# Sliding-window attention: block-diagonal scores in the tile mode of the values, and both next to each other

## The chip, the cores and the metric

The kernel runs on one core of one Trainium2 chip. The metric is the device time of one execution, in microseconds (us); less is better. The granted TensorE clock is 1.00. Repeated executions of one kernel mostly agree within about 0.1%.

## The reference

Four blocks follow each other: attention, feed-forward over tokens, and both again. Only the attention matters here. It has 2048 positions, 32 heads of 32 elements, and every query sees eight keys: its own position and the seven at distance 2, 4, ... 14 before it.

```python
def _A_ref(x, wqkv, wo):
    H = 32; Dh = D // H
    W, dil = 8, 2
    q, k, v = ...                        # x @ wqkv, split into heads
    idx = pos[:, None] - (jnp.arange(W) * dil)[None, :]
    kg, vg = k[:, :, idx_c, :], v[:, :, idx_c, :]      # the 8 keys and values of each query
    logits = jnp.einsum("bhsd,bhswd->bhsw", q, kg) * Dh ** -0.5     # masked where idx < 0
    o = jnp.einsum("bhsw,bhswd->bhsd", _softmax(logits), vg)
    return o.reshape(B, S, D) @ wo

x = x + _A_ref(_layernorm(x), A_wqkv, A_wo)
x = x + _B_ref(_layernorm(x), ...)       # feed-forward; then both once more
```

## The kernel before

Positions are split into even and odd ones (`c`), so that the eight keys of a query are neighbours. Four heads (`g`) and one parity make a unit `u`, 16 units per layer; half a unit is a *visit*, 32 visits per layer, numbered 0 to 31. In each visit TensorE computes the scores of half a unit, the values (probabilities times v, and their row sums) of the half unit before it, and two of the four 512-column chunks of q or k of the next unit. In visits 30 and 31 there is no next unit, and two output projections each take the place of the chunks.

TensorE's order within a visit is fixed by the program:

```python
for vis in range(2 * NU):
    u, b = divmod(vis, 2)
    ...                                             # cut: weight loads
    in_order(scores, u, b)
    for n in range(2):
        if n and vis:
            in_order(values, *divmod(vis - 1, 2), v, oT)
        if u + 1 < NU:
            in_order(qk_chunk, u + 1, wts, *chunks[2 * b + n])
        else:
            in_order(out_proj, 0, 2 * b + n, oT, wo, res, xa[li], h2)
in_order(values, NU - 1, 1, v, oT)
for c, i in order[4:]:
    out_proj(c, i, oT, wo, res, xa[li], h2)
```

The scores use array tiles of 32 rows by 64 columns: 32 rows since a head has 32 elements, 64 keys, 72 queries. The values use tiles of 128 rows (keys) by 32 columns (elements of a head). The chunks and projections use the whole array.

```python
def scores(u, b):
    ...
    for i in range(HB):
        for r in range(2):
            for h in range(HG):                     # one head per row tile
                mm = nc.tensor.matmul(ss[h // 2][r * HK:(r + 1) * HK, h % 2, i * HW:(i + 1) * HW],
                                      lhsT=k[hp, lo:lo + HK], rhs=q[hp, lo:lo + HW], start=True, stop=True)
    for n in range(2):
        nc.scalar.activation(out=pc[...], in_=ss[n][:, :, 0:HB * HW], func=ACT.Exp, scale=scale, bias=shift[:])
    for r in range(2):                              # keep the band, write it into Pm
        nc.vector.tensor_tensor(out=pm[rp, :, ...], in0=pc[rp], in1=mk, op=ALU.mult)

def values(u, b, v, oT):
    acc = a_tile()                                  # one buffer of two PSUM banks
    ...                                             # cut: matmuls of v and of ones with Pm, into acc
    nc.scalar.activation(out=rd[:], in_=acc[:, 1, :], func=ACT.Ln)
    nc.scalar.activation(out=rd[:], in_=rd[:], func=ACT.Exp, scale=-1.0)
    nc.vector.tensor_tensor(out=oT[g][...], in0=acc[:, 0, :], in1=rd[:], op=ALU.mult)   # frees acc

def qk_chunk(u, wts, part, n):
    ...                                             # cut: eight matmuls of 128x512 into ps
    if n == 0: nc.scalar.copy(out=dst[:, lo:lo + 512], in_=ps[:])
    else:      nc.vector.tensor_copy(out=dst[:, lo:lo + 512], in_=ps[:])

def out_proj(c, i, oT, wo, res, dst, h2):
    xr = x2("xr")
    nc.sync.dma_start(out=xr[:], in_=res(c, i))     # the residual
    xn = x2("xn")
    for n in range(NDC):
        ...                                         # cut: eight matmuls of 128x512 into ps (two buffers in all)
        nc.vector.tensor_tensor(out=xn[:, xs_], in0=ps[:], in1=xr[:, xs_], op=ALU.add)   # frees ps
    nc.sync.dma_start(out=rows(dst, c, i), in_=xn[:])
    ...                                             # cut: statistics (VectorE), normalisation (ScalarE)
```

PSUM has `m` tiles (two buffers of one bank, for chunks and projections), `s` tiles (two of two banks, scores) and `acc` (one of two banks, values).

The softmax here doesn't subtract the row's maximum and nothing guards it: scores larger than these inputs give would overflow.

Of the kernel before, what the change touches and what calls it, by code (L numbers as in the profile page):

```python
# [14 lines left out]
P = 128  # L15
H = 32
DH = 32
# [8 lines left out]
def kernel(  # L26
# [31 lines left out]
    NW2 = 4  # L58
    HF = FT // NW2
    KW = P + W  # L60
    HK = P // 2
    HW = HK + W
    PAD = W
    SHIFT = 14.0
    assert D == H * DH and NT == 16 and NI == 8 and NG == 8 and HG == 4
    scale = float(DH) ** -0.5
# [20 lines left out]
    def s_tile():  # L87
        return pss.tile([P, 2, 512], FP32, name="s", tag="s")
# [13 lines left out]
    def x2(name, shape=None, dt=BF16):  # L102
        return x2p.tile(shape or [P, D], dt, name=name, tag="x2")
# [18 lines left out]
    nc.vector.memset(shift[:], -SHIFT)  # L122
    ones = const.tile([P, DH], BF16, name="ones")
    nc.vector.memset(ones[:], 1.0)
    band = const.tile([P, HW], BF16, name="band")
    nc.gpsimd.memset(band[:], 1.0)
    for r in range(2):
        hb_ = band[r * HK:(r + 1) * HK]
        nc.gpsimd.affine_select(out=hb_, in_=hb_, compare_op=ALU.is_ge, fill=0.0, base=0,
                                pattern=[[1, HW]], channel_multiplier=-1)  # L130
        nc.gpsimd.affine_select(out=hb_, in_=hb_, compare_op=ALU.is_ge, fill=0.0, base=W - 1,
                                pattern=[[-1, HW]], channel_multiplier=1)
    b1_bf = const.tile([P, FT], BF16, name="b1_bf")
    b2_bf = const.tile([P, NI, DIL], BF16, name="b2_bf")
    b1_sb = const.tile([P, FT], FP32, name="b1_sb")
# [9 lines left out]
        return nc.vector.tensor_copy(out=b2_sb[:], in_=b2_bf[:])  # L145

    hT = pers.tile([P, KD, S], BF16, name="hT")
    qT = [pers.tile([P, S + PAD], BF16, name=f"qT{n}") for n in range(2)]
    kT = [pers.tile([P, S], BF16, name=f"kT{n}") for n in range(2)]
    Pm = [pers.tile([P, HG, NI, KW], BF16, name=f"Pm{n}") for n in range(2)]  # L150
    def zero_fill():
        for t in qT:
            nc.vector.memset(t[:, S:S + PAD], 0.0)
        for t in Pm:
            nc.vector.memset(t[0:HK, :, :, HW:KW], 0.0)
            r = nc.vector.memset(t[HK:P, :, :, 0:HK], 0.0)
        return r

    xa = [dram.tile([S, D], BF16, name=f"xa{li}") for li in range(2)]
# [187 lines left out]
    def qk_chunk(u, wts, part, n):  # L347
        g, c = divmod(u, DIL)
        ps = m_tile()
        lo = c * SC + n * 512  # L350
        for kt in range(KD):
            mm = nc.tensor.matmul(ps[:], lhsT=wts[part][:, kt, (g % 2) * P:(g % 2 + 1) * P], rhs=hT[:, kt, lo:lo + 512],  # L352
                                  start=(kt == 0), stop=(kt == KD - 1))
        dst = (qT, kT)[part][g % 2]
        if n == 0:
            nc.scalar.copy(out=dst[:, lo:lo + 512], in_=ps[:])
        else:
            nc.vector.tensor_copy(out=dst[:, lo:lo + 512], in_=ps[:])
        return mm

    last_pe = [None]
# [2 lines left out]
        with tc.issue_after(last_pe[0].ins) if last_pe[0] is not None else nullcontext():  # L364
            last_pe[0] = f(*args)

    HB = NI // 2

    def scores(u, b):
        g, c = divmod(u, DIL)  # L370
        q, k, pm = qT[g % 2], kT[g % 2], Pm[u % 2]
        ss = [s_tile() for _ in range(2)]
        for i in range(HB):
            for r in range(2):
                lo = c * SC + (b * HB + i) * P + r * HK
                for h in range(HG):
                    hp = slice(h * DH, (h + 1) * DH)
                    mm = nc.tensor.matmul(ss[h // 2][r * HK:(r + 1) * HK, h % 2, i * HW:(i + 1) * HW],  # L378
                                          lhsT=k[hp, lo:lo + HK], rhs=q[hp, lo:lo + HW], start=True, stop=True)
        pc = pcp.tile([P, HG, HB, HW], BF16, name="pc", tag="pc")  # L380
        for n in range(2):
            nc.scalar.activation(out=pc[:, 2 * n:2 * n + 2].rearrange("p h t k -> p h (t k)"), in_=ss[n][:, :, 0:HB * HW],  # L382
                                 func=ACT.Exp, scale=scale, bias=shift[:])
        for r in range(2):
            rp = slice(r * HK, (r + 1) * HK)
            mk = band[rp].unsqueeze(1).unsqueeze(1).to_broadcast([HK, HG, HB, HW])
            nc.vector.tensor_tensor(out=pm[rp, :, b * HB:(b + 1) * HB, r * HK:r * HK + HW], in0=pc[rp], in1=mk, op=ALU.mult)  # L387
        return mm

    def values(u, b, v, oT):  # L390
        g, c = divmod(u, DIL)
        pm = Pm[u % 2]
        acc = a_tile()
        hb = NI // 2
        t0 = b * hb
        for i in range(-1 if b else 0, hb):
            t = t0 + i
            for h in range(HG):
                hp = slice(h * DH, (h + 1) * DH)
                lhs = v[c][t][:, g * P + h * DH:g * P + (h + 1) * DH]  # L400
                if i < 0:
                    nc.tensor.matmul(acc[hp, 0, 0:W], lhsT=lhs, rhs=pm[:, h, t, P:KW], start=True, stop=False,
                                     skip_group_check=True)
                else:
                    w = KW if i < hb - 1 else P
                    nc.tensor.matmul(acc[hp, 0, i * P:i * P + w], lhsT=lhs, rhs=pm[:, h, t, 0:w],  # L406
                                     start=(t == 0), stop=(i == hb - 1), skip_group_check=True)
        for h in range(HG):
            hp = slice(h * DH, (h + 1) * DH)
            nc.tensor.matmul(acc[hp, 1, :].rearrange("p (t q) -> p t q", q=P), lhsT=ones[:], rhs=pm[:, h, t0:t0 + hb, 0:P],  # L410
                             start=True, stop=False, skip_group_check=True)
        s0 = t0 - 1 if b else 0
        ns = t0 + hb - 1 - s0
        o0 = (s0 + 1 - t0) * P
        for h in range(HG):
            hp = slice(h * DH, (h + 1) * DH)
            dst = acc[hp, 1, :].rearrange("p (t q) -> p t q", q=P)[:, o0 // P:o0 // P + ns, 0:W]
            mm = nc.tensor.matmul(dst, lhsT=ones[:], rhs=pm[:, h, s0:s0 + ns, P:KW], start=False, stop=True,
                                  skip_group_check=True)
        rd = x2("rd", [P, 512], FP32)  # L420
        nc.scalar.activation(out=rd[:], in_=acc[:, 1, :], func=ACT.Ln)
        nc.scalar.activation(out=rd[:], in_=rd[:], func=ACT.Exp, scale=-1.0)  # L422
        lo = c * SC + t0 * P
        nc.vector.tensor_tensor(out=oT[g][:, lo:lo + hb * P], in0=acc[:, 0, :], in1=rd[:], op=ALU.mult)  # L424
        return mm

    def load_wo():
# [99 lines left out]
    for li in range(2):  # L527
        first = li == 0
        v = [[None] * NI for _ in range(DIL)]
        for c, i in order:  # L530
            v[c][i] = vhp.tile([P, D], BF16, name="v", tag="vh")
        wv = load_wv()
        if first:
            start_up(v, wv)
            wts = [None, None]
            chain_("SP", load_qk, 0, wts)
            res = lambda c, i: xin_v[c, i]
        else:
            fill_wv(wv, 0)
            fill_wv(wv, 1)  # L540
            wts = [None, None]
            load_qk(0, wts)
            for i in range(NI):
                for c in range(DIL):
                    v_proj(v, c, i, wv, (0, 1))
            res = lambda c, i: rows(xb, c, i)
        oT = [gop.tile([P, S], BF16, name="oT", tag="go") for _ in range(NG)]
        h2 = [[None] * NI for _ in range(DIL)]
        chunks = [(0, 0), (0, 1), (1, 0), (1, 1)]
        last_pe[0] = None  # L550
        for part, n in chunks:
            in_order(qk_chunk, 0, wts, part, n)
        wo = None
        for vis in range(2 * NU):
            u, b = divmod(vis, 2)
            if b == 0 and u + 1 < NU and (u + 1) % (2 * DIL) == 0:
                wts = [None, None]
                load_qk((u + 1) // (2 * DIL), wts)
            if vis == 2 * NU - 6:
                wo = load_wo()  # L560
            in_order(scores, u, b)
            for n in range(2):
                if n and vis:
                    in_order(values, *divmod(vis - 1, 2), v, oT)
                if u + 1 < NU:
                    in_order(qk_chunk, u + 1, wts, *chunks[2 * b + n])
                else:
# [4 lines that stand above are left out]
        g = [None] * NFB  # L572
        for fb in range(NFB):
            gemm1(fb, h2, g)
        if first:
            ln_exp_table()
        for i in range(NI):
            w2t = load_w2(i)
            for c in range(DIL):
                gemm2(c, i, w2t, g, xa[li], rows(xb, c, i) if first else out_v[c, i], first)  # L580
# [30 lines left out]
```

## Time and profile before

Median 1300.6 us of three runs (1300.58 to 1300.79). From the page of the profile, busy time of each engine, and below it the chain of work that ended last. PE is TensorE, PEld its weight loads, DVE VectorE, ACT ScalarE, POOL GpSimd, and SPq the queue of SyncE; a number after x is a count.

```profile
PE 1279.1 (99%) x9240; PEld 582.0 (45%) x9398; DVE 392.9 (30%) x654; ACT 386.0 (30%) x628; POOL 1.7 (0%) x11
...
PE 96%; DVE 2%; issue 1%; ACT 0%; DMA 0%; SPq 0%; another core or an unknown queue 0%
```

TensorE is the limit everywhere. What can be gained in attention is not idle time, for there is hardly any in the records, but the time that TensorE spends between matmuls. To see it, read the starts in the timeline. This is one visit, TensorE alone; the columns are start (us), duration of the piece (us), engine, line, operation, output and inputs, and the number of instructions.

```profile
152.98 0.38 PE L352 MATMUL m<-hT,wqk 128*128 128x512 bf16 x1
153.29 0.34 PE L378 MATMUL s<-qT,kT 32*64 32x72 bf16 x32
153.78 1.67 PE L352 MATMUL m<-hT,wqk 128*128 128x512 bf16 x7 [0.16 <-issue]
155.39 0.19 PE L402 MATMUL acc<-Pm,v 128*32 128x8 bf16 x4
...
155.99 1.90 PE L352 MATMUL m<-hT,wqk 128*128 128x512 bf16 x8
157.82 0.34 PE L378 MATMUL s<-qT,kT 32*64 32x72 bf16 x32
```

L378 is the scores, L352 a chunk, L402 the first line of the values. From scores to scores this visit takes 4.53 us; the mean of visits 1 to 28 is 4.5216 us. (The first of the eight matmuls at 153.78 is one of the few records missing from the trace.) Matmuls of a chunk start 216 ns apart, but the scores start 0.31 us after the last matmul of the chunk before them (152.98 to 153.29), and so do the values: 93 ns are lost each time TensorE goes from the whole array into small tiles. Coming back costs a similar time: in the next visit, where that record is there, the last score matmul and the next chunk start 126 ns apart, though groups of eight scores follow each other every 33 ns, and the last ones start only 9 to 11 ns after the last matmul of the group before. The Trainium skill, "TensorEngine Tiling (Array Packing)", Tiling Modes, says that changing the tiling mode drains the array. A visit enters and leaves small tiles twice.

The groups of VectorE (DVE) and ScalarE (ACT) in the stage: after the shapes come the count, busy us, mean ns of one, and the idle time before them with its cause.

```profile
L387 DVE TENSOR_TENSOR Pm<-pc,band 64x1152 bf16<-64x1152 bf16 x128 | 96.2, 752 | 65.1 <-ACT pc L382 63.1
...
L424 DVE TENSOR_TENSOR oT<-acc,rd 128x512 bf16<-128x512 f32 x64 | 44.0, 687 | 39.7 <-ACT rd L422 39.7
...
L358 DVE CAST qT<-m 128x512 bf16<-128x512 f32 x32 | 21.8, 682 | 75.4 <-PE m L352 75.4
```

VectorE has two masks, one oT and one cast in a visit, about 2.9 of 4.52 us, and it waits for others: there is slack.

### The profile page before, as it was taken

The page shows a single profiled execution, that of the slowest core. Times are in us where ns is not written, and L with a number is a line of the kernel's source. Part 1 is how long each engine was busy: PE and PEld are TensorE (multiplying, and loading weights), DVE is VectorE, ACT ScalarE, POOL GpSimd, SP SyncE. Part 2 cuts the span into 40 slices and gives each one's busy share as a digit, 9 for nine tenths or more (in the row PEclk, how much of TensorE's full clock was granted, in tenths as well). Part 3 has the DMA queues.
Part 4 walks back from the last instruction along what each step waited for, and adds up shares of the span by engine and source line. Part 5 has one row for each costly group of instructions (what it writes and reads, how often), then busy time and mean ns, then how long its engine had stood idle before and what let it go on. Part 6 is the DMA issues. An engine that isn't in the chain of part 4 may idle for free.

```text
span 1298.5 us, 20885 instructions
## 1 busy us (share of the span) xinstructions
PE 1279.1 (99%) x9240; PEld 582.0 (45%) x9398; DVE 392.9 (30%) x654; ACT 386.0 (30%) x628; POOL 1.7 (0%) x11
## 2 busy tenths in 40 slices
PE   9999999999999999999999999999999999999998
PEld 4444444444444444444444444444444444444443
DVE  7346667820000022322300666688000000111111
ACT  5457666521111110000023677765211111000000
POOL 0000000000000000000000000000000000000000
PEclk9999999999999999999999999999999999999999
DMA  8620113443222235555432100044422222334320
GB/s 236 133 77 21 35 34 111 150 145 91 65 80 77 57 105 143 130 154 140 130 81 65 35 21 27 24 145 157 129 65 84 78 59 80 104 106 140 112 91 33
DMA packets 195818, 121.69 MB, mean 94 GB/s; under 512 B 37904, under 2 KB 177424, under 8 KB 195728
## 3 DMA queue, kind: packets, MB, share of 16 engines
q1 hardware_dynamic: 195728, 120.36, 32.7%
q8 instruction: 73, 1.20, 0.4%
q14 instruction: 17, 0.14, 0.0%
HBM read 96.48 MB, written 16.78 MB: 87 GB/s over the span
## 4 chain that ended last, share of the span: by engine, by line
PE 96%; DVE 2%; issue 1%; ACT 0%; DMA 0%; SPq 0%; another core or an unknown queue 0%
PE m L352 17%; PE s L515 15%; PE s L472 15%; PE acc L472 7%; PE m L472 7%; PE m L515 7%; PE acc L515 7%; PE m L445 7%; PE m L337 4%; PE m L255 4%; PE acc L406 1%; PE s L378 1%; PE acc L410 1%; DVE xn L447 1%; DVE bn L180 0%
## 5 line engine op out<-in xcount | busy, mean ns | idle before, releaser
L472 PEld LDWEIGHTS <-w 128*128 128x128 bf16 x1792 | 175.4, 98 | 211.4
L515 PEld LDWEIGHTS <-w 128*128 128x128 bf16 x1792 | 175.3, 98 | 211.4
L352 PE MATMUL m<-hT,wqk 128*128 128x512 bf16 x963 | 231.0, 380 | 7.9 <-issue 7.0
L472 PE MATMUL s<-h,w 128*128 128x512 bf16 x878 | 201.3, 379 | 0.8
L515 PE MATMUL s<-g,w 128*128 128x512 bf16 x884 | 199.3, 379 | 0.7
L518 DVE SCALAR_TENSOR_TENSOR xo<-s,b_sb,xs 128x512 bf16<-128x512 f32 x32 | 24.0, 751 | 540.7 <-PE s L515 529.1
L352 PEld LDWEIGHTS <-wqk 128*128 128x128 bf16 x1024 | 90.5, 98 | 108.7 <-issue 12.9
L387 DVE TENSOR_TENSOR Pm<-pc,band 64x1152 bf16<-64x1152 bf16 x128 | 96.2, 752 | 65.1 <-ACT pc L382 63.1
L445 PE MATMUL m<-wo,oT 128*128 128x512 bf16 x498 | 111.5, 379 | 0.9
L382 ACT ACTIVATE pc<-s,shift 128x576 bf16<-128x576 f32 x128 | 87.8, 737 | 59.9 <-PE s L378 59.9
L472 PE MATMUL acc<-h,w 128*128 128x512 bf16 x440 | 103.1, 379 | 0.5
L515 PE MATMUL acc<-g,w 128*128 128x512 bf16 x436 | 99.6, 379 | 0.5
L472 PE MATMUL m<-h,w 128*128 128x512 bf16 x438 | 98.5, 379 | 0.5
L515 PE MATMUL m<-g,w 128*128 128x512 bf16 x436 | 98.3, 379 | 0.6
L174 ACT ACTIVATE ln<-mv,eps 128x1 f32<-128x1 f32 x64 | 18.9, 295 | 227.5 <-DVE mv L182 222.2
L479 ACT ACTIVATE g<-s,b_sb 128x1024 bf16<-128x1024 f32 x28 | 31.2, 1114 | 166.9 <-PE s L472 155.2
L445 PEld LDWEIGHTS <-oT 128*128 128x128 bf16 x512 | 49.4, 98 | 59.7 <-issue 1.3
L255 PE MATMUL m<-wv,hT 128*128 128x512 bf16 x250 | 55.6, 379 | 1.0 <-ACT hT L249 0.7
L424 DVE TENSOR_TENSOR oT<-acc,rd 128x512 bf16<-128x512 f32 x64 | 44.0, 687 | 39.7 <-ACT rd L422 39.7
L337 PE MATMUL m<-wv,hT 128*128 128x512 bf16 x251 | 55.2, 379 | 0.3
L447 DVE TENSOR_TENSOR xn<-m,xr 128x512 bf16<-128x512 f32 x64 | 44.0, 688 | 8.0 <-PE m L445 6.5
L180 DVE BATCH_NORM_STATS2 bn<-xn 128x6 f32<-128x512 bf16 x64 | 44.4, 693 | 1.4
(59 smaller groups left out, 604.9 us busy)
## 6 DMA issues: line engine op xcount, KB each, us to landing
w<-in_B_w_dram SPq DMA_DIRECT2D x56, 512.0 KB, 3.8
w<-in_B_w_dram SPq DMA_DIRECT2D x64, 448.0 KB, 4.7
wqk<-in_A_wqkv_dram SPq DMA_DIRECT2D x16, 512.0 KB, 5.9
xa<-xn SPq DMA_DIRECT2D x32, 256.0 KB, 2.0
xs<-xa SPq DMA_DIRECT2D x32, 256.0 KB, 3.2
wv<-in_A_wqkv_dram SPq DMA_DIRECT2D x8, 512.0 KB, 5.6
wo<-in_A_wo_dram SPq DMA_DIRECT2D x8, 512.0 KB, 4.9
xr<-in_A_x_dram SPq DMA_DIRECT2D x16, 256.0 KB, 2.9
```

Of the source, the lines that this page charges most:

```text
L180: nc.vector.bn_stats(out=s[:, cc, :], in_=x[:, cc * 512:(cc + 1) * 512])
L255: r = nc.tensor.matmul(pss_[k, n][:], lhsT=hT[:, kt, cols(*order[k])], rhs=wv[n][kt // 4][:, kt % 4, :], start=(kt == 0), stop=(kt == KD - 1))
L337: nc.tensor.matmul(ps[:], lhsT=hT[:, kt, cols(c, i)], rhs=wv[n][kt // 4][:, kt % 4, :], start=(kt == 0), stop=(kt == KD - 1))
L352: mm = nc.tensor.matmul(ps[:], lhsT=wts[part][:, kt, (g % 2) * P:(g % 2 + 1) * P], rhs=hT[:, kt, lo:lo + 512], start=(kt == 0), stop=(kt = ...
L382: nc.scalar.activation(out=pc[:, 2 * n:2 * n + 2].rearrange("p h t k -> p h (t k)"), in_=ss[n][:, :, 0:HB * HW], func=ACT.Exp, scale=scale ...
L387: nc.vector.tensor_tensor(out=pm[rp, :, b * HB:(b + 1) * HB, r * HK:r * HK + HW], in0=pc[rp], in1=mk, op=ALU.mult)
L424: nc.vector.tensor_tensor(out=oT[g][:, lo:lo + hb * P], in0=acc[:, 0, :], in1=rd[:], op=ALU.mult)
L445: mm = nc.tensor.matmul(ps[:], lhsT=oT[g][:, cols(c, i)], rhs=wo[n][g // 4][:, g % 4, :], start=(g == 0), stop=(g == NG - 1))
L447: nc.vector.tensor_tensor(out=xn[:, xs_], in0=ps[:], in1=xr[:, xs_], op=ALU.add)
L472: nc.tensor.matmul(pairs[fl][0][dc], lhsT=wt[c][:, i, fl * P:(fl + 1) * P], rhs=h2[c][i][:, dc * 512:(dc + 1) * 512], start=(k == 0), stop ...
L479: nc.scalar.activation(out=g[fb][:, fl, :].rearrange("p (n d) -> p n d", n=2), in_=t[:], func=ACT.Gelu_apprx_tanh, bias=b1_sb[:, ft:ft + 1])
L515: nc.tensor.matmul(aps[dc], lhsT=w2t[ft // HF][:, ft % HF, c::DIL], rhs=g[ft // GF][:, ft % GF, dc * 512:(dc + 1) * 512], start=(ft == 0), ...
```

## The change

Its intent: give the scores the tile mode of the values, so that both can be done in one go and a visit changes mode once each way, not twice. For that the contraction must run over all 128 rows. q is written block-diagonally, head h in partitions 32h to 32h+31 of its own block with zeros elsewhere, and one matmul of 32 keys by 4x40 queries gives the scores of four heads. The price is four copies for each q chunk, four masks for two, and an eviction of every chunk by ScalarE. The scores of a half unit now take 640 columns of PSUM, not 1152.

```diff
+    qB = [pers.tile([P, HG, SC + W], BF16, name=f"qB{n}") for n in range(2)]     # zero outside the diagonal
+    Pm = pers.tile([P, HG, NS * HB, KW], BF16, name="Pm")                        # three half units in turn
 def qk_chunk(...):
-        if n == 0:
-            nc.scalar.copy(out=dst[:, lo:lo + 512], in_=ps[:])
+        if part:
+            nc.scalar.copy(out=kT[u % 2][:, ls], in_=ps[:])
         else:
-            nc.vector.tensor_copy(out=dst[:, lo:lo + 512], in_=ps[:])
+            qs = x2("qs", [P, 512])
+            nc.scalar.copy(out=qs[:], in_=ps[:])
+            for h in range(HG):
+                nc.vector.tensor_copy(out=qB[u % 2][hp, h, ls], in_=qs[hp, :])
 def scores(u, b):
+            for r in range(P // KG):                                             # KG = 32, GW = 40
+                mm = nc.tensor.matmul(dst, lhsT=k[:, lo + r * KG:lo + (r + 1) * KG],
+                                      rhs=q[:, :, lo + r * KG:lo + r * KG + GW], start=True, stop=True)
+        nc.scalar.activation(out=pc[...], in_=ss[:, :, 0:2 * HG * GW], func=ACT.Exp, ...)
+        for r in range(P // KG):
+            nc.vector.tensor_tensor(out=Pm[rp, ...], in0=pc[rp], in1=mk, op=ALU.mult)
 # cut: the outputs in scores (dst, pc, rp), the indices of Pm in values, the old scores
 for vis in range(2 * NU):
             in_order(scores, u, b)
+            if vis:
+                in_order(values, *divmod(vis - 1, 2), v, oT)
             for n in range(2):
-                if n and vis:
-                    in_order(values, *divmod(vis - 1, 2), v, oT)
                 if u + 1 < NU:
                     in_order(qk_chunk, u + 1, wts, *chunks[2 * b + n])
                 else:
                     in_order(out_proj, 0, 2 * b + n, oT, wo, res, xa[li], h2)
```

More of the change, by code (lines that the diff above doesn't have):

```diff
@@ L60 @@
     KW = P + W
-    HK = P // 2
-    HW = HK + W
-    PAD = W
+    KG = 32
+    GW = KG + W
+    HB = NI // 2
+    NS = 3
     SHIFT = 14.0
@@ L124 @@
     nc.vector.memset(ones[:], 1.0)
-    band = const.tile([P, HW], BF16, name="band")
+    band = const.tile([P, GW], BF16, name="band")
     nc.gpsimd.memset(band[:], 1.0)
-    for r in range(2):
-        hb_ = band[r * HK:(r + 1) * HK]
+    for r in range(P // KG):
+        hb_ = band[r * KG:(r + 1) * KG]
         nc.gpsimd.affine_select(out=hb_, in_=hb_, compare_op=ALU.is_ge, fill=0.0, base=0,
-                                pattern=[[1, HW]], channel_multiplier=-1)
+                                pattern=[[1, GW]], channel_multiplier=-1)
         nc.gpsimd.affine_select(out=hb_, in_=hb_, compare_op=ALU.is_ge, fill=0.0, base=W - 1,
-                                pattern=[[-1, HW]], channel_multiplier=1)
+                                pattern=[[-1, GW]], channel_multiplier=1)
     b1_bf = const.tile([P, FT], BF16, name="b1_bf")
@@ L147 @@
     hT = pers.tile([P, KD, S], BF16, name="hT")
-    qT = [pers.tile([P, S + PAD], BF16, name=f"qT{n}") for n in range(2)]
-    kT = [pers.tile([P, S], BF16, name=f"kT{n}") for n in range(2)]
-    Pm = [pers.tile([P, HG, NI, KW], BF16, name=f"Pm{n}") for n in range(2)]
+    qB = [pers.tile([P, HG, SC + W], BF16, name=f"qB{n}") for n in range(2)]
+    kT = [pers.tile([P, SC], BF16, name=f"kT{n}") for n in range(2)]
+    Pm = pers.tile([P, HG, NS * HB, KW], BF16, name="Pm")
     def zero_fill():
-        for t in qT:
-            nc.vector.memset(t[:, S:S + PAD], 0.0)
-        for t in Pm:
-            nc.vector.memset(t[0:HK, :, :, HW:KW], 0.0)
-            r = nc.vector.memset(t[HK:P, :, :, 0:HK], 0.0)
+        nc.vector.memset(Pm[:].rearrange("p h t k -> p (h t k)"), 0.0)
+        for t in qB:
+            r = nc.vector.memset(t[:].rearrange("p h t -> p (h t)"), 0.0)
         return r
@@ L353, in qk_chunk @@
                                   start=(kt == 0), stop=(kt == KD - 1))
-        dst = (qT, kT)[part][g % 2]
-        if n == 0:
-            nc.scalar.copy(out=dst[:, lo:lo + 512], in_=ps[:])
-        else:
-            nc.vector.tensor_copy(out=dst[:, lo:lo + 512], in_=ps[:])
+        ls = slice(n * 512, (n + 1) * 512)
+        if part:
+            nc.scalar.copy(out=kT[u % 2][:, ls], in_=ps[:])
+        else:
+            qs = x2("qs", [P, 512])
+            nc.scalar.copy(out=qs[:], in_=ps[:])
+            for h in range(HG):
+                hp = slice(h * DH, (h + 1) * DH)
+                nc.vector.tensor_copy(out=qB[u % 2][hp, h, ls], in_=qs[hp, :])
         return mm
@@ L365, in in_order @@
             last_pe[0] = f(*args)
-    HB = NI // 2
     def scores(u, b):
-        g, c = divmod(u, DIL)
-        q, k, pm = qT[g % 2], kT[g % 2], Pm[u % 2]
-        ss = [s_tile() for _ in range(2)]
+        q, k = qB[u % 2], kT[u % 2]
+        s0 = (2 * u + b) % NS * HB
+        ss = s_tile()
         for i in range(HB):
-            for r in range(2):
-                lo = c * SC + (b * HB + i) * P + r * HK
-                for h in range(HG):
-                    hp = slice(h * DH, (h + 1) * DH)
-                    mm = nc.tensor.matmul(ss[h // 2][r * HK:(r + 1) * HK, h % 2, i * HW:(i + 1) * HW],
-                                          lhsT=k[hp, lo:lo + HK], rhs=q[hp, lo:lo + HW], start=True, stop=True)
-        pc = pcp.tile([P, HG, HB, HW], BF16, name="pc", tag="pc")
-        for n in range(2):
-            nc.scalar.activation(out=pc[:, 2 * n:2 * n + 2].rearrange("p h t k -> p h (t k)"), in_=ss[n][:, :, 0:HB * HW],
-                                 func=ACT.Exp, scale=scale, bias=shift[:])
-        for r in range(2):
-            rp = slice(r * HK, (r + 1) * HK)
-            mk = band[rp].unsqueeze(1).unsqueeze(1).to_broadcast([HK, HG, HB, HW])
-            nc.vector.tensor_tensor(out=pm[rp, :, b * HB:(b + 1) * HB, r * HK:r * HK + HW], in0=pc[rp], in1=mk, op=ALU.mult)
+            lo = (b * HB + i) * P
+            for r in range(P // KG):
+                rp = slice(r * KG, (r + 1) * KG)
+                dst = ss[rp, i // 2, i % 2 * HG * GW:(i % 2 + 1) * HG * GW].rearrange("p (h k) -> p h k", k=GW)
+                mm = nc.tensor.matmul(dst, lhsT=k[:, lo + r * KG:lo + (r + 1) * KG],
+                                      rhs=q[:, :, lo + r * KG:lo + r * KG + GW], start=True, stop=True)
+        pc = pcp.tile([P, HB, HG, GW], BF16, name="pc", tag="pc")
+        nc.scalar.activation(out=pc[:].rearrange("p (n t) h k -> p n (t h k)", n=2), in_=ss[:, :, 0:2 * HG * GW],
+                             func=ACT.Exp, scale=scale, bias=shift[:])
+        for r in range(P // KG):
+            rp = slice(r * KG, (r + 1) * KG)
+            mk = band[rp].unsqueeze(1).unsqueeze(1).to_broadcast([KG, HB, HG, GW])
+            nc.vector.tensor_tensor(out=Pm[rp, :, s0:s0 + HB, r * KG:r * KG + GW].rearrange("p h t k -> p t h k"),
+                                    in0=pc[rp], in1=mk, op=ALU.mult)
         return mm
@@ L391, in values @@
         g, c = divmod(u, DIL)
-        pm = Pm[u % 2]
         acc = a_tile()
-        hb = NI // 2
-        t0 = b * hb
-        for i in range(-1 if b else 0, hb):
+        t0 = b * HB
+        s0 = (2 * u + b) % NS * HB
+        sp = (s0 - 1) % (NS * HB)
+        for i in range(-1 if b else 0, HB):
             t = t0 + i
@@ L401, in values @@
                 if i < 0:
-                    nc.tensor.matmul(acc[hp, 0, 0:W], lhsT=lhs, rhs=pm[:, h, t, P:KW], start=True, stop=False,
+                    nc.tensor.matmul(acc[hp, 0, 0:W], lhsT=lhs, rhs=Pm[:, h, sp, P:KW], start=True, stop=False,
                                      skip_group_check=True)
                 else:
-                    w = KW if i < hb - 1 else P
-                    nc.tensor.matmul(acc[hp, 0, i * P:i * P + w], lhsT=lhs, rhs=pm[:, h, t, 0:w],
-                                     start=(t == 0), stop=(i == hb - 1), skip_group_check=True)
+                    w = KW if i < HB - 1 else P
+                    nc.tensor.matmul(acc[hp, 0, i * P:i * P + w], lhsT=lhs, rhs=Pm[:, h, s0 + i, 0:w],
+                                     start=(t == 0), stop=(i == HB - 1), skip_group_check=True)
         for h in range(HG):
             hp = slice(h * DH, (h + 1) * DH)
-            nc.tensor.matmul(acc[hp, 1, :].rearrange("p (t q) -> p t q", q=P), lhsT=ones[:], rhs=pm[:, h, t0:t0 + hb, 0:P],
+            nc.tensor.matmul(acc[hp, 1, :].rearrange("p (t q) -> p t q", q=P), lhsT=ones[:], rhs=Pm[:, h, s0:s0 + HB, 0:P],
                              start=True, stop=False, skip_group_check=True)
-        s0 = t0 - 1 if b else 0
-        ns = t0 + hb - 1 - s0
-        o0 = (s0 + 1 - t0) * P
-        for h in range(HG):
-            hp = slice(h * DH, (h + 1) * DH)
-            dst = acc[hp, 1, :].rearrange("p (t q) -> p t q", q=P)[:, o0 // P:o0 // P + ns, 0:W]
-            mm = nc.tensor.matmul(dst, lhsT=ones[:], rhs=pm[:, h, s0:s0 + ns, P:KW], start=False, stop=True,
-                                  skip_group_check=True)
+        runs = [(s0, HB - 1, 1)]
+        if b:
+            runs = [(sp, HB, 0)] if sp < s0 else [(sp, 1, 0)] + runs
+        for lo_, n_, t_ in runs:
+            for h in range(HG):
+                hp = slice(h * DH, (h + 1) * DH)
+                dst = acc[hp, 1, :].rearrange("p (t q) -> p t q", q=P)[:, t_:t_ + n_, 0:W]
+                mm = nc.tensor.matmul(dst, lhsT=ones[:], rhs=Pm[:, h, lo_:lo_ + n_, P:KW], start=False, stop=True,
+                                      skip_group_check=True)
         rd = x2("rd", [P, 512], FP32)
@@ L423, in values @@
         lo = c * SC + t0 * P
-        nc.vector.tensor_tensor(out=oT[g][:, lo:lo + hb * P], in0=acc[:, 0, :], in1=rd[:], op=ALU.mult)
+        nc.vector.tensor_tensor(out=oT[g][:, lo:lo + HB * P], in0=acc[:, 0, :], in1=rd[:], op=ALU.mult)
         return mm
```

## The prediction

> **What bounds the kernel now.** TensorE: the page's busy table gives PE 99%, the chain that ended last is 96% PE, granted clock 1.00. In attention the timeline shows one visit (scores, q/k chunk, values, q/k chunk) every 4.51 to 4.54 us, 64 visits in two layers, about 290 us. Matmul starts within a visit: sixteen 128x512 projections 216 ns apart (3.45 us); into each of the two small-tile stages the distance is 309 ns, so 93 ns extra twice; scores to next projection 268 ns (four groups of eight, 33 ns apart, then 126 ns from the last small matmul to the projection); values to projection 578 to 606 ns. The Trainium skill, "TensorEngine Tiling (Array Packing)", Tiling Modes, says that changing the mode drains the array; the 309 against 216 ns agrees.
>
> **What changes on TensorE.** Scores take the 128x32 mode of values and sit next to them: one entry (93 ns), one leaving drain (about 90 ns) and a 10 ns wobble go. Scores become 16 matmuls of 160 columns, four at a time. Values' 136-column groups start 59 ns apart, so I estimate 69 ns per group, 276 ns, against about 176 ns of streaming now. Net gain about 95 ns per visit, 4.52 to 4.43 us: 6 us in all (0.45%).
>
> **What changes elsewhere.** ACT: exp columns fall from 2x576 (737 ns each) to one 640 (estimate 790 ns), but it now evicts both chunks (586 ns each): 3.2 of 4.43 us, harmless. DVE: two masks of 64x1152 (752 ns, 781 ns apart) become four of 32x640. 752 ns is 600 ns at two elements per cycle plus 150, so estimate 485 ns, 516 ns apart: 2.06 us instead of 1.54. Its chunk cast (682 ns per visit) goes, but each q chunk needs four 32x512 copies. The Trainium skill, "VectorE: DVE Perf Modes", the perf-mode tier table, gives bf16 SBUF copies four elements per cycle; here 128x1024 and 128x512 normalisations (546 and 404 ns) have that slope. Estimate 295 ns, 325 apart, 1.3 us per chunk. Both q chunks fall in visit b=0, so DVE has about 8.0 us of work per pair of visits of 8.86 us, and bunched.
>
> **Critical path.** Following the queues with these durations: chunk-1 copies run until 2.3 us into visit b=1, its masks until 4.4, then oT, ending about 0.65 us into the next visit. The single accumulator (one buffer) is released only then, while values want it at 0.28 us. Stall 0.2 to 0.5 us per pair, settling near 0.2 because a delayed PE lets DVE catch up: about 6 us over 31 pairs. This nearly eats the gain. The two visits with output projection are DVE-heavy already (adds, statistics), perhaps 1 us more per layer. Start-up zero fills grow but lie in DVE's 19 us of idle time.
>
> **Prediction.** 1300 us, range 1294 to 1308 (8 in 10). Faster by over 2%: 1%; within 2%: 94%; slower by over 2%: 5%.
>
> **What would show it.** Two 309 ns entries per visit become one; score groups 69 ns apart; no drain between scores and values; masks near 485 ns, q copies near 295; DVE busy near 8 us per pair; before values of b=0 visits a PE gap over 0.1 us, released by the oT multiply. Without it: about 1295.
>
> **What would make it wrong.** Copies or masks not in their fast modes (copies at one element per cycle cost 3 us per pair more: about 60 us slower); rhs in 40-column pieces streaming slower than 69 ns per group; DVE's instruction order putting oT before the masks, which removes the stall; score weight loads not hidden.

## More of the kernel before

Last, SyncE's queue where visits 29 to 31 of the first layer lie (visit 30 starts at 207.55):

```profile
203.14 0.37 SPq L460 DMA_DIRECT2D w<-in_B_w_dram  x1
203.63 0.50 SPq L439 DMA_DIRECT2D xr<-in_A_x_dram  x1
207.65 0.37 SPq L460 DMA_DIRECT2D w<-in_B_w_dram  x1
208.52 0.35 SPq L439 DMA_DIRECT2D xr<-in_A_x_dram  x1
213.05 0.34 SPq L448 DMA_DIRECT2D xa<-xn  x1
213.50 0.38 SPq L439 DMA_DIRECT2D xr<-in_A_x_dram  x1
216.75 0.33 SPq L448 DMA_DIRECT2D xa<-xn  x1
```

The first residual (xr) is under way four microseconds before the first projection, and then one store (xa) and one load alternate. No TensorE wait for a residual is on the list of waits.

The tiles `xr`, `xn` and `rd` share six buffers. One thing is not in the source as such: the order in which the instructions of SyncE's queue, stores and loads alike, stand in the compiled program. SyncE takes them in that order.

## The result

The changed kernel takes 1305.46 us (1305.33 to 1305.6, four runs) against 1300.59: ratio 1.0037, 95% interval 1.002 to 1.0055. Ratios here are the mean time of one kernel's fast runs over that of the other's of the same rounds, so not quite the ratio of the medians quoted. It is 5 us slower, and those are distinct from the noise. The page of after:

```profile
PE 1278.7 (98%) x8258; PEld 592.9 (45%) x8414; DVE 454.4 (35%) x971; ACT 372.4 (29%) x628; POOL 2.4 (0%) x15
...
PE 95%; DMA 2%; DVE 2%; issue 1%; ACT 1%; DVEq 0%; SPq 0%
```

DMA has come into the chain with 2%: something that did not hold anything up now does. To find where the time went, the trace is cut at the first score matmul of visits 0, 30 and 31 of each layer, and at the first matmul of the second feed-forward product (FF2). All in us:

| stretch | before | after | difference |
|---|---|---|---|
| start to visit 0 | 72.61 | 72.58 | -0.03 |
| visits 0 to 29, layer 1 | 134.94 | 133.65 | -1.29 |
| visit 30 | 7.99 | 9.41 | +1.42 |
| visit 31 to FF2 | 243.52 | 246.71 | +3.19 |
| FF2 to visit 0 of layer 2 | 255.64 | 255.64 | 0 |
| visits 0 to 29, layer 2 | 134.94 | 133.66 | -1.28 |
| visit 30 | 7.99 | 9.45 | +1.46 |
| visit 31 to FF2 | 243.52 | 245.16 | +1.64 |
| FF2 to end | 197.35 | 197.34 | -0.01 |

So the visits gained 2.6 us, and the two stage ends lost 7.7. The change pays where it was made to pay and loses more at a place that it touches only in passing.

**The visits.** Mean of visits 1 to 28: 4.4745 us, against 4.5216. Two visits that follow each other differ: one of each pair has a wait in it, and this is that one. TensorE alone (L380 is the scores, L404 and the lines after it the values):

```profile
161.17 0.38 PE L352 MATMUL m<-hT,wqk 128*128 128x512 bf16 x1
161.48 0.46 PE L380 MATMUL s<-qB,kT 128*32 128x160 bf16 x16
161.88 0.19 PE L404 MATMUL acc<-Pm,v 128*32 128x8 bf16 x4
...
162.71 3.40 PE L352 MATMUL m<-hT,wqk 128*128 128x512 bf16 x15 [0.16 <-issue]
```

The entry of 0.31 us stands there once, before the scores, and none before the values: the scores' groups start 69 to 70 ns apart, as estimated. But from scores to values there are 0.40 us (161.48 to 161.88). In the visit before it, it is 0.29 (157.07 to 157.36): in every second visit TensorE waits, here for 0.11 us. (Over the visits of this kind in the trace the wait is 0.02 to 0.22 us, in the mean 0.08.) What for is to be seen on VectorE at the same time:

```profile
160.61 0.49 DVE L388 TENSOR_TENSOR Pm<-pc,band 32x640 bf16<-32x640 bf16 x1
161.13 0.69 DVE L427 TENSOR_TENSOR oT<-acc,rd 128x512 bf16<-128x512 f32 x1
```

The oT multiply, which frees the only accumulator, runs from 161.13 to 161.82, right behind the last mask, and the values start at 161.88. The list of waits does not show this one; the order of the times does, and a run below tests it. The groups of VectorE:

```profile
L388 DVE TENSOR_TENSOR Pm<-pc,band 32x640 bf16<-32x640 bf16 x256 | 123.7, 483 | 46.0 <-ACT pc L383 39.2
L362 DVE COPY qB<-qs 32x512 bf16<-32x512 bf16 x256 | 72.6, 284 | 77.5 <-ACT qs L359 73.4
L427 DVE TENSOR_TENSOR oT<-acc,rd 128x512 bf16<-128x512 f32 x64 | 44.2, 691 | 3.2 <-ACT rd L425 1.4
```

Masks of 483 ns and copies of 284 ns are what the prediction estimated (485 and 295). The idle time before oT has fallen from 39.7 to 3.2 us: it used to wait for ScalarE, and now it waits for its turn. It is a sign that is easily missed, for VectorE's share of the whole span is only 35%.

**The stage ends.** From the list of waits of after, with total us, number and longest wait:

```profile
PE m L448 <- DVE xn L450: 7.3, 6, 2.0
...
DVE xn L450 <- DMA xr<-in_A_x_dram: 4.2, 4, 2.6
...
DVE xn L450 <- DMA xr<-xb: 2.5, 3, 1.0
```

Neither pair is on the list of before. TensorE waits for the add that frees a projection's PSUM tile, and the add waits for the residual. SyncE's queue tells why the residual is late (visit 30 starts at 206.22):

```profile
201.91 4.78 SPq L463 DMA_DIRECT2D w<-in_B_w_dram  x2
206.80 1.38 SPq L442 DMA_DIRECT2D xr<-in_A_x_dram  x2
213.39 3.40 SPq L451 DMA_DIRECT2D xa<-xn  x2
216.88 0.89 SPq L442 DMA_DIRECT2D xr<-in_A_x_dram  x2
```

The first residual used to stand between two weight loads of the feed-forward; now it stands behind both. The second of these, a prefetch that nobody is waiting for, goes out only when visit 30 begins: SyncE waits 4.3 us for TensorE before it, and by the program what it waits for is the buffer of weights that the last chunk of visit 29 has just used. So the residual is issued at 206.80, not 203.6. The transfer itself, which runs beside a weight load in both kernels, took hardly longer, 4.43 us from issue to landing against 4.05 before: it is late because it is issued late. And stores and loads come in pairs now: the third residual waits until the store of the second projection can go, which is until that projection has been added up. At the first of these waits, with the residual's arrival as its end:

```profile
211.35 0.69 DVE L450 TENSOR_TENSOR xn<-m,xr 128x512 bf16<-128x512 f32 x1 [0.96 <-DMA xr<-in_A_x_dram]
212.07 0.69 DVE L180 BATCH_NORM_STATS2 bn<-xn 128x6 f32<-128x512 bf16 x1
212.09 3.61 PE L448 MATMUL m<-wo,oT 128*128 128x512 bf16 x16 [1.31 <-DVE xn L450]
```

### The profile page after: what moved, and what is told of

Its sections match the earlier page's. It is cut to its first block, busy times and chain, and to the rows that moved or that the text cites. A ratio compares the mean times of both kernels' runs of the same rounds, so it can differ in the third digit from the quotient of the medians.

```text
span 1303.6 us, 19189 instructions
## 1 busy us (share of the span) xinstructions
PE 1278.7 (98%) x8258; PEld 592.9 (45%) x8414; DVE 454.4 (35%) x971; ACT 372.4 (29%) x628; POOL 2.4 (0%) x15
## 4 chain that ended last, share of the span: by engine, by line
PE 95%; DMA 2%; DVE 2%; issue 1%; ACT 1%; DVEq 0%; SPq 0%
PE m L352 17%; PE s L518 15%; PE s L475 15%; PE acc L475 7%; PE m L475 7%; PE m L518 7%; PE acc L518 7%; PE m L448 6%; PE m L337 4%; PE m L255 4%; PE s L380 2%; PE acc L408 1%; DMA xr<-in_A_x_dram 1%; PE acc L412 1%; DMA xr<-xb 1%
## 5 line engine op out<-in xcount | busy, mean ns | idle before, releaser
L352 PE MATMUL m<-hT,wqk 128*128 128x512 bf16 x963 | 223.4, 379 | 6.2 <-issue 4.6
L352 PEld LDWEIGHTS <-wqk 128*128 128x128 bf16 x1024 | 95.2, 98 | 118.0 <-issue 10.7
L388 DVE TENSOR_TENSOR Pm<-pc,band 32x640 bf16<-32x640 bf16 x256 | 123.7, 483 | 46.0 <-ACT pc L383 39.2
L362 DVE COPY qB<-qs 32x512 bf16<-32x512 bf16 x256 | 72.6, 284 | 77.5 <-ACT qs L359 73.4
L359 ACT CAST qs<-m 128x512 bf16<-128x512 f32 x64 | 37.5, 585 | 51.4 <-PE m L352 50.3
L383 ACT ACTIVATE pc<-s,shift 128x640 bf16<-128x640 f32 x64 | 51.1, 799 | 0.0
L356 ACT CAST kT<-m 128x512 bf16<-128x512 f32 x64 | 37.5, 585 | 46.5 <-PE m L352 46.5
```

What stands on the lines that cost most here:

```text
L352: mm = nc.tensor.matmul(ps[:], lhsT=wts[part][:, kt, (g % 2) * P:(g % 2 + 1) * P], rhs=hT[:, kt, lo:lo + 512], start=(kt == 0), stop=(kt = ...
L356: nc.scalar.copy(out=kT[u % 2][:, ls], in_=ps[:])
L359: nc.scalar.copy(out=qs[:], in_=ps[:])
L362: nc.vector.tensor_copy(out=qB[u % 2][hp, h, ls], in_=qs[hp, :])
L383: nc.scalar.activation(out=pc[:].rearrange("p (n t) h k -> p n (t h k)", n=2), in_=ss[:, :, 0:2 * HG * GW], func=ACT.Exp, scale=scale, bia ...
L388: nc.vector.tensor_tensor(out=Pm[rp, :, s0:s0 + HB, r * KG:r * KG + GW].rearrange("p h t k -> p t h k"), in0=pc[rp], in1=mk, op=ALU.mult)
```

## The experiments

The theories on the stage ends. H: the order in SyncE's queue, which comes from two projections following each other. D: VectorE has too much to do there (four masks, oT, adds and statistics); this is the reason that the prediction gave. Q: the new qs tiles hold buffers of the pool from which the residuals take theirs. On the visits, S: the single accumulator is freed late. Each run had five rounds (four fast runs counted for the one in old order with new scores), and the kernel before ran on the same chip with 1300.3 to 1300.5 us as its median. "Stage ends" are given as visit 30 / visit 31 to FF2.

| run | us | ratio | visit | ends, layer 1 | ends, layer 2 |
|---|---|---|---|---|---|
| before | 1300.6 | | 4.5216 | 7.99 / 243.52 | 7.99 / 243.52 |
| after | 1305.46 | 1.0037 | 4.4745 | 9.41 / 246.71 | 9.45 / 245.16 |
| e1_end_order | 1302.17 | 1.0014 | 4.4753 | 8.11 / 245.79 | 8.11 / 245.17 |
| e2_before_new_order | 1301.57 | 1.0009 | 4.4150 | 9.29 / 245.72 | 10.38 / 244.47 |
| e3_acc2 | 1304.13 | 1.0029 | 4.4296 | 10.69 / 245.95 | 9.23 / 245.29 |
| e4_xr_queue | 1300.07 | 1.0000 | 4.4751 | 8.36 / 244.22 | 8.36 / 244.23 |
| f1_before_mid_order | 1294.04 | 0.9952 | 4.4150 | 7.99 / 243.52 | 7.99 / 243.51 |
| f2_end_order_qs_pool | 1302.11 | 1.0012 | 4.4739 | 8.11 / 245.76 | 8.11 / 245.16 |
| f4_new_scores_old_order | 1312.13 | 1.0093 | 4.6489 | 8.11 / 245.63 | 8.11 / 245.22 |
| f5_acc2_xr_queue | 1297.72 | 0.9979 | 4.4296 | 8.36 / 244.23 | 8.36 / 244.22 |
| g1_end_order_xr_queue | 1298.77 | 0.9987 | 4.4741 | 8.11 / 243.83 | 8.11 / 243.83 |
| g2_before_new_order_xr_queue | 1294.89 | 0.9957 | 4.4150 | 8.35 / 243.47 | 8.35 / 243.47 |

"us" is the median; the last three columns are from the one profiled execution. All results were correct.

### e1_end_order: the old order in visits 30 and 31 alone

```diff
-            if vis:
+            if vis and u + 1 < NU:
                 in_order(values, *divmod(vis - 1, 2), v, oT)
             for n in range(2):
+                if n and u + 1 == NU:
+                    in_order(values, *divmod(vis - 1, 2), v, oT)
```

> The changed kernel, but in the last two visits of each layer (those with output projections) the values stand between the two projections again, as before the change. Theory H (the loss at the end of each attention stage comes from the order of the DMA queue: the first residual load stands behind a weight load that waits, and two loads stand behind two stores): the two stage ends give back nearly all of the 7.7 us they lost, time 1297.5 to 1299, no PE gap over 1 us among output projections. Theory D (VectorE is overloaded there by four masks, oT and the projections' adds and statistics, as predicted): nothing is given back, 1305. Theory Q (the new qs tiles take buffers from the residual tiles' pool): nothing is given back, since qs is still in that pool. Visits before the end: 4.474 us as in the changed kernel.

Half a hit. Visit 30 fell to 8.11 us, but from visit 31 on 2.3 and 1.7 us too much remained, and 1302.17 us lies between the theories' numbers. Neither H as put nor D or Q as put holds; runs f2 and g1 take up what is left. (In this run's queue the first residual again stands before the second weight load, but the second one goes out at 212.44, behind the first store at 211.99; in the kernel before it went out at 208.52.)

### e2_before_new_order: the kernel before, with only the new order

The loop is changed as in the change; scores, masks and casts stay the old ones.

> The kernel before with its own scores (32x64 mode), masks and casts, only the order of a visit is the new one: scores, values, two projections. Theory H: the same two stage-end losses as in the changed kernel (about 7.7 us in all) appear although DVE has no q copies and only two masks; the queue order is the same. Theory D and Q: no loss there. Visits: if what counts is the number of entries into small-tile stages, one 93 ns entry goes and scores to values costs a switch of about 126 ns, so 4.42 us per visit and no accumulator stall; if the shared mode is what counts, 4.5 us. Time by H: 1302 to 1307; by D or Q: 1294 to 1299.

The stage ends lose 6.8 us in all, without a single q copy and with two masks, not four: D and Q cannot be the main cause. SyncE's queue shows the same pairs as after:

```profile
200.37 4.77 SPq L460 DMA_DIRECT2D w<-in_B_w_dram  x2
205.25 1.38 SPq L439 DMA_DIRECT2D xr<-in_A_x_dram  x2
211.72 3.40 SPq L448 DMA_DIRECT2D xa<-xn  x2
```

The visits hold the surprise. With the old scores, in a mode other than the values', they take 4.4150 us, less than with the new ones:

```profile
160.21 0.38 PE L352 MATMUL m<-hT,wqk 128*128 128x512 bf16 x1
160.52 0.34 PE L378 MATMUL s<-qT,kT 32*64 32x72 bf16 x32
160.79 0.19 PE L402 MATMUL acc<-Pm,v 128*32 128x8 bf16 x4
```

From scores to values there are 0.27 us although the mode changes there; with the new scores, which change no mode, it is 0.29 us at best. The last score matmul and the first value matmul start 123 ns apart, just as far as the last score matmul and a chunk (126 ns) before: a step from one small mode into another costs one drain, and no second entry. The time of 1301.57 us lies half a microsecond under the range expected, the ends having lost 6.8 us and not 7.7.

### e3_acc2: two accumulators

```diff
-    pss = pool("pss", 2, space=bass.MemoryType.PSUM)
-    psa = pool("psa", 1, space=bass.MemoryType.PSUM)
+    pss = pool("pss", 1, space=bass.MemoryType.PSUM)
+    psa = pool("psa", 2, space=bass.MemoryType.PSUM)
     # and the transposes at the start and one more of the four feed-forward tiles take acc for s
```

> The changed kernel with two accumulator buffers for values and one score buffer instead of one and two. Theory S (in every second visit the values wait 0.11 us for the single accumulator, which the oT multiply frees late because q copies and four masks stand before it on DVE): all visits become 4.41 to 4.43 us, the gap of 170 ns between the last score matmul and the first value matmul becomes 59 ns, and the time falls by 3 to 3.5 us to about 1302. Rival (the masks themselves are what values wait for, or a DVE that is too slow on average): visits stay at 4.47 us on average, 1305.

S holds: 4.4296 us per visit, from scores to values 0.29 us in both kinds of visit, while VectorE's busy time is the same (454.4 us in both). The kind of visit that waited:

```profile
160.60 0.46 PE L380 MATMUL s<-qB,kT 128*32 128x160 bf16 x16
160.89 0.18 PE L404 MATMUL acc<-Pm,v 128*32 128x8 bf16 x4
```

The wait was worth 0.045 us per visit, 1.3 us per layer. The time fell by 1.3 us, not by 3: the runs of this kernel spread from 1303.15 to 1306.06, and in the profiled one visit 30 took 10.69 us in the first layer. TensorE arrives earlier at the late residuals; its waits for the adds are 7.8 us on the list of waits, against 7.3 in the changed kernel.

### e4_xr_queue: the residual loads issued from GpSimd's queue

```diff
-        nc.sync.dma_start(out=xr[:], in_=res(c, i))
+        nc.gpsimd.dma_start(out=xr[:], in_=res(c, i))
```

> The changed kernel with the residual loads of the output projections issued from GpSimd's DMA queue instead of SyncE's, everything else the same. Theory H: the first residual load no longer waits behind the feed-forward weight load nor behind stores, most of the 7.7 us at the stage ends comes back, 1298 to 1300.5. Theory D or Q: 1305.

H holds for most of the loss: 5.4 us come back (1305.46 to 1300.07), and 5.6 us of the 7.7 at the ends. (Four of the five runs lie between 1299.69 and 1300.22; one took 1301.82 us, of which the traced span explains 0.6.) The add no longer waits for a residual anywhere on the list of waits. The Trainium skill, "DMA: Bandwidth & Descriptors", Issuing engines are not separate DMA queues, says that initiating DMAs on several engines will "only save the time on the sequencer it takes to initiate the DMA". Here it saved far more, since what the load escaped was the wait of another transfer before it in the same engine's program. What is left is of another kind. VectorE in visit 31 of this run:

```profile
216.45 1.97 DVE L388 TENSOR_TENSOR Pm<-pc,band 32x640 bf16<-32x640 bf16 x4 [0.21 <-ACT pc L383]
218.46 0.22 DVE L192 TENSOR_SCALAR bi<-mv,rs 128x1 f32<-128x1 f32 x1
218.59 0.68 DVE L427 TENSOR_TENSOR oT<-acc,rd 128x512 bf16<-128x512 f32 x1
219.19 0.68 DVE L450 TENSOR_TENSOR xn<-m,xr 128x512 bf16<-128x512 f32 x1
```

Masks, oT and add stand behind each other without a pause, and TensorE waits for the add: here D acts.

### f2_end_order_qs_pool: e1, with a pool of its own for qs

```diff
+    qsp = pool("qsp", 2)
-            qs = x2("qs", [P, 512])
+            qs = qsp.tile([P, 512], BF16, name="qs", tag="qs")
```

> The changed kernel with the old order in the last two visits, and with the qs tiles in a pool of their own. It is for the 4 us that the old order did not give back. Theory Q (qs tiles hold buffers that the residual loads need): the second residual load comes earlier, 1298. Theory H: the queue's order is unchanged, the second residual load still stands behind the first store, 1302.

1302.11 us and the ends as in e1: Q falls.

### g1_end_order_xr_queue: e1, with the residuals on GpSimd's queue

The edit of e4 on the kernel of e1.

> The changed kernel with the old order in the last two visits and the residual loads on GpSimd's queue. The old order alone gave back the time of visit 30 but left 2.2 us after visit 31 in the first layer and 1.6 in the second. Theory H (there too a residual load stands behind a store in SyncE's queue): visit 30 near 8.0 us, and from visit 31 to the second feed-forward product 243.5 to 244; 1298 to 1299. Theory D (what is left is VectorE's load by the new scores): 245 to 246 there, 1302.

1298.77 us, and 243.83 us from visit 31 on. So it was the queue that held back most of the rest of e1, too: in its program the second residual stands behind the first store, as it does not in the kernel before. From e1 to g1 the ends give back 3.3 us. This loss does not come from two projections following each other, for e1 has the old order at the ends. It comes with the new scores: f4, which has the old order throughout, shows the same ends as e1, and f1, with the old scores, does not. What in the new scores moved the load behind the store in the compiled program was not found; f2 shows only that it is not the pool of qs.

### f4_new_scores_old_order: the new scores without the new order

The loop of before in the changed kernel.

> The changed kernel with the old order of every visit (scores, projection, values, projection), so the new scores without the adjacency. Theory: four switches as before, scores 0.07 to 0.1 us longer, no accumulator stall since values come 2 us later in the visit: visits of 4.59 to 4.62 us, 2.2 to 3 us per layer slower than before, stage ends as in the run with the old end order (4 us lost), 1308 to 1311. Rival (the shared mode saves something by itself, or the new scores are cheaper): visits at or under 4.52 us.

4.6489 us per visit, somewhat more than expected (4.62), and 1312.13 us (expected at most 1311): the new scores cost TensorE 0.127 us per visit, not up to 0.1. From the first score to the next chunk there are 0.39 us in this run (160.73 to 161.12), against 0.27 in the kernel before (157.82 to 158.09). In the old order the new scores alone are a loss.

### f1_before_mid_order: the old scores, the new order in visits 0 to 29

The loop of e1 in the kernel before, and nothing else:

```diff
+            if vis and u + 1 < NU:
+                in_order(values, *divmod(vis - 1, 2), v, oT)
             for n in range(2):
-                if n and vis:
+                if n and u + 1 == NU:
                     in_order(values, *divmod(vis - 1, 2), v, oT)
```

> The kernel before with its own scores, masks and casts; scores, values, two projections in the first 30 visits of a layer, the old order in the last two. If the gain of the change is the adjacency alone (one entry of 93 ns less per visit) and its loss at the stage ends is the order of the queue there: visits of 4.415 us, stage ends as before (7.99 us for visit 30, 243.5 us from visit 31 to the second feed-forward product), time 1294 to 1295, faster than every other version. If the old scores in the new order bring a loss of their own: 1297 or more.

A hit: 1294.04 us (1293.8 to 1294.56), ratio 0.9952 with an interval of 0.994 to 0.9965. It is the fastest version found, 6.3 us under the kernel before and 11.4 under the change, with two lines added and one changed. SyncE's queue is again the one of before:

```profile
200.56 0.50 SPq L439 DMA_DIRECT2D xr<-in_A_x_dram  x1
204.47 0.37 SPq L460 DMA_DIRECT2D w<-in_B_w_dram  x1
205.35 0.35 SPq L439 DMA_DIRECT2D xr<-in_A_x_dram  x1
```

### f5_acc2_xr_queue and g2_before_new_order_xr_queue

The first is e3 and e4 together, the best of the new scores with the new order throughout; the second is e2 with the residuals on GpSimd's queue.

> The changed kernel with two accumulators and one score buffer, and the residual loads on GpSimd's queue: both losses taken away. Visits 4.43 us, stage ends as in the run with that queue (8.4 and 244.2 us): 1297 to 1298. If the two losses aren't independent (the freed PE only meets another wait): 1299 to 1300.

> The kernel before with the new order in all visits and the residual loads on GpSimd's queue. Visits 4.415 us. Theory H: the stage ends fall from 9.3 to 10.4 and 244.5 to 245.7 us to at most the 8.36 and 244.2 us of the changed kernel with that queue; 1295 to 1297. If VectorE's load is what is left there, they fall to 8.0 and 243.5: 1294 to 1295, since this kernel has two masks and no q copies.

The first: 1297.72 us, as expected; the two losses are independent. The second: 1294.89 us. With it the ends can be split. Of the two kernels with the new order and the separate queue, e4 has the new scores and takes 244.22 us after visit 31; g2 has the old ones and takes 243.47. So 0.75 us per layer come with the new scores. TensorE's waits for the adds, in e4 and then in g2, with total us, number and longest wait, differ by as much, 1.4 us in two layers:

```profile
PE m L448 <- DVE xn L450: 2.0, 4, 0.8
```

```profile
PE m L445 <- DVE xn L447: 0.6, 2, 0.3
```

The add follows masks and oT there without a pause, so this is D's share. In visit 30 the two take 8.36 and 8.35 us against 7.99 of before, so these 0.37 us come with the order. TensorE waits there for an add in both, for 0.25 us in e4 and 0.31 in g2; the rest was not taken apart.

## Why the prediction was right, and where it was not

The time, 1305.46 us, lies within the range of 1294 to 1308, and "within 2%" was right. The estimate was 1300. The hit is in part luck, as the sum at the end of this section shows. Taken apart:

- **TensorE's gain, about 95 ns per visit.** Right in size: without the wait for the accumulator the visit takes 4.4296 us (e3) against 4.5216, 92 ns less. Of the signs named, one entry for two, groups of 69 ns and no drain before the values are all in the trace. (VectorE's busy time was 7.4 to 7.5 us per pair of visits, not near 8.) But the prediction booked the shared mode as the source. The four kinds of visit (before and f4; f1 and e3) say otherwise:

| us per visit | old order | new order, no accumulator wait |
|---|---|---|
| old scores (32x64) | 4.5216 | 4.4150 |
| new scores (128x32) | 4.6489 | 4.4296 |

  Putting scores and values next to each other saves 107 ns with the old scores, in two different modes, and 219 ns with the new ones, in one mode. So the shared mode is worth some 112 ns more (by subtraction; e3 also has one score buffer less); the new scores cost 127 ns. The two nearly cancel, and the whole net gain could be had from the order alone.

- **The accumulator, "stall 0.2 to 0.5 us per pair".** Right in mechanism: every second visit, behind masks and copies, ended by oT, and gone with a second accumulator. The size was 0.11 us per pair by the starts of one pair (0.40 less 0.29 us). By the means it is 2 x (4.4745 - 4.4296) = 0.09 us, less than half of what was predicted: about 2.7 us in all, not 6. The copies are a little faster than estimated (284 ns, and 298 from start to start in the median, not 295 and 325), which over eight copies gives VectorE back 0.2 us per pair. The Trainium skill, "VectorE: DVE Perf Modes", Two Vector instructions with no wait between them, says that an instruction whose inputs or output start in another group of 32 partitions than those of the one before is held until the earlier ones are done. The trace agrees: a mask of 480 ns and the next one, in other partitions, start 511 ns apart, while the copy behind an oT of 691 ns, in the same group, starts after 609.

- **The stage ends, "perhaps 1 us more per layer".** This is the term that was wrong. It measured 4.6 us in the first layer and 3.1 in the second. The reason given, VectorE's load, is real and makes 0.75 us per layer. But 5.6 us of the 7.7 come from SyncE's queue: a residual load now waits behind a prefetch, and loads wait behind stores (e4 takes it away). Two things moved the loads there, and either is enough for a loss. One is that two projections came to follow each other (e2 shows 6.8 us at the ends with the old scores). The other comes with the new scores, even with the old order at the ends: it cost 3.3 us from e1 to g1, and why it does so stays open. The prediction asked what each engine has to do there, and not in which order the loads stand and what each one ahead of them waits for.

The prediction's own terms add up to about 1302.6 us (6 us gained, 6 us of stalls, 2 us at the ends); the estimate was set a little below its own sum. From there to 1305.5 the errors partly offset each other: the stalls were taken to be 3.3 us too large, the gain about half a microsecond too large, and the loss at the ends 5.7 us too small. Had the stalls been as large as predicted, the time would have been about 1308.8 us by this sum, just outside the range: that the number came out right rests on one error covering part of another.

## What to carry to other kernels

Before rebuilding a small matmul to share a tile mode with its neighbour, move it next to its neighbour as it is: here the step between the two small modes (123 ns between starts) cost as much as one return to the whole array (126 ns), and the order alone gave all of the gain. When the order of work or the work itself changes, read the queue of loads and stores again in the compiled program: a transfer that nobody is waiting for may now stand before one that everybody is waiting for. And look at the idle time before the instruction that frees a single buffer: when it falls to nearly nothing (here from 39.7 to 3.2 us), the engine that was never the limit may have become part of the path, whatever its share of the span.

## What the Trainium skill lacked or had wrong

- "TensorEngine Tiling (Array Packing)", Tiling Modes, says that changing the mode drains the array but gives no price. Here going from the whole array into small tiles put 93 ns more between two starts (309 and 216 ns), and leaving the 32x64 scores left 126 ns between the last of them and the next chunk, where groups of them follow each other every 33.
- The same sentence makes no difference between leaving the whole array and a step from one small mode to another. Here, from 32x64 to 128x32, it put 123 ns between the starts: once the price of leaving, with no entry on top.
- No page tells that a short contraction can be filled up with zeros to keep the column mode, nor its price: 16 matmuls of 160 columns, groups of four 69 to 70 ns apart, for 32 of 72 columns, groups of eight 33 ns apart; 127 ns more per visit where TensorE's order is the same (f4 and before).
- "DMA: Bandwidth & Descriptors", Issuing engines are not separate DMA queues, names the sequencer's time to initiate a DMA as the only gain of issuing from several engines, and leaves out a load that stands behind a waiting transfer. Here the second issuing engine gave 5.4 us (1305.46 to 1300.07), since a load left the queue in which it stood behind such a transfer.
- "VectorE: DVE Perf Modes", Two Vector instructions with no wait between them, has the rule but no times: here a held mask started 31 ns after the end of the mask before it (511 and 480 ns), a held copy behind a copy 14 ns after that end (297 and 283 ns), and a copy that is not held 82 ns before the end of the oT (609 and 691 ns).
